# Linear attention and two feed-forward layers on one core: a new order of the second products, copies and accumulating transfers dealt out anew

## The chip, the core and the metric

The kernel runs on one core of a Trainium2 chip, in one launch. The metric is the time of an execution on the device in microseconds (us), lower is better. "Before" and "after" are the same program but for the change below. Engines are named as the profile names them: PE is the matrix engine (PEld its weight loads), DVE the vector engine, ACT the scalar engine, POOL and SP the other two; PSUM is the memory that PE writes its products to, SBUF the on-chip working memory.

## The reference

```
kv  = einsum('bhsd,bhse->bhde', k, v)          # B=8, H=8, S=576, D=64
att = einsum('bhsd,bhde->bhse', q, kv)
x   = att / sqrt(mean(att^2) + 1e-6) * g_norm  # -> x: 4608 tokens x 512
h   = x @ w_in ; x = (relu(h)^2) @ w_out       # layer 1: 512 -> 2048 -> 512
h   = x @ w_in2; out = (h * cos(h)) @ w_out2   # layer 2: 512 -> 2048 -> 512
```

All inputs and the output are float32; the four weight matrices come as 64-bit floats, read as pairs of 32-bit words and rebuilt as float32 on the chip.

## The kernel before

**Numbers in two parts.** A float32 operand of a large product is split into a rounded high part h (an ACT cast) and a low part l (a DVE subtraction). A product is then three matmuls: h·h, h·l and l·h.

**Two phases.** In the first phase (`run_chunks`, 72 chunks) attention is computed and half of layer 1's hidden width goes through plain products (L379, L416); the partial results go to memory as `p_d` through `evict` (L402, L404). All this time the weights of the rest are rebuilt (`load_w`, `conv_steps`), combined and written back to memory as `wi_d` and `ws_d`. The rest, half of layer 1 (m=0) and all of layer 2 (m=1), runs in the second phase (`run_slots`) as 30 **slots** (m, t, q): t is one of five token tiles (twice 512, 512, 512, 384, 384 tokens), q a group of hidden columns (2 groups in layer 1, 4 in layer 2). Slots 0 to 9 are layer 1, 10 to 29 layer 2; slots 6 to 9 and 22 to 29 have the narrow tiles of 384.

**Seven products instead of eight.** Each slot does a 2x2 block product with seven multiplications twice: seven **first products** (`first_product`, L508, input times w_in, banks FA and FB) and, after the activation (`relu_*` or `cos_*`), seven **second products** (`second_product`, L631, activation times w_out, banks SA and SB). Sums that several result blocks share are built in PSUM by leaving a bank standing: with the products called 0 to 6, block (0,0) is 0+1, (1,1) is 0+3+2+5, (0,1) is 0+3+2+4, (1,0) is 0+3+5+6. Products 0, 3, 5, 6 use one bank pair, 1, 2, 4 the other; which is SA and which SB alternates from slot to slot (`s_bank`).

**Second products before.** The order is `S_ORDER` = 0, 1, 3, 2, 5, 4, 6. In a "seeded" slot (26 of 30, `seeded_s`) product 0 isn't added to its result block; ACT copies its bank into the other bank (L650) and product 1 accumulates on top of that. `drain_product` takes the sums out of PSUM into the block's running sum in SBUF: by an ACT copy where the sum starts (L654), by a DVE addition (L662), or, in layer 2 but for the last slot, for the products in `BY_DMA` = 4, 5, 1, 6 by an ACT copy into a tile `part` (L659, pool `t`, two buffers) and an **accumulating transfer** issued from POOL's queue (L660).

**What sets the order.** Everything is emitted by one planner: `at(position, function, ...)` puts a step at a position counted in slots, `PH` = 1/7 slot being one product's place. First products of slot k run at k to k+1, second products at k+1.25 to k+2.25, one matmul of each in turn. `s_block` prepares the operand of second product i 1.6 places ahead (differences on DVE at L591, cast L607 on ACT, low part L608 on DVE); `x_block` does the same for the first products (L463, L481, L482), once per tile, around the start of slots with q=0; `late_stream` places seven conversions of layer 2's weights ("pairs": L111 to L125, L175, L192, L194). Each engine does its instructions in the order in which they were emitted. A tile waits until the earlier tile in the same place has been used; the pools of the second phase (`c`, `t`, `late`) lie where buffers of the first phase were.

Of the kernel before, what the change touches and what calls it, by code (L numbers as in the profile page):

```python
# [8 lines left out]
F32 = mybir.dt.float32  # L9
# [13 lines left out]
def kernel(  # L23
# [105 lines left out]
    def load_w(kind, m, f, i):  # L129
        if kind == "seven":  # L130
            raw = pools["raw"].tile([P, 4, P, 2], U32, tag="raw", name="raw")
            for df, places in ((0, (1, 0)), (1, (2, 3))):
                src = (wA, wB)[m][2 * f + df, :, 1, :].rearrange("p (c n) -> p c n", n=2 * P)
                for d, place in enumerate(places):
                    nc.sync.dma_start(out=raw[:, place].rearrange("p n two -> p (n two)"), in_=src[:, 2 * d + i, :])
        elif kind == "pair":
            raw = pools["raw"].tile([P, 4, P, 2], U32, tag="raw", name="raw")
            for df, dst in ((0, raw[:, 1:3]), (1, raw[:, 0::3])):
                src = (wA, wB)[m][2 * f + df, :, 0, :].rearrange("p (c n) -> p c n", n=2 * P)
                nc.sync.dma_start(out=dst.rearrange("p k n two -> p k (n two)"), in_=src[:, i::2, :])  # L140
        elif kind == "pairs":
            raw = pools["raw"].tile([P, 4, 2 * P, 2], U32, tag="raw", name="raw")
            for df, dst in ((0, raw[:, 1:3]), (1, raw[:, 0::3])):
                src = (wA, wB)[m][2 * f + df, :, 0, :].rearrange("p (k n) -> p k n", n=4 * P)
                nc.sync.dma_start(out=dst.rearrange("p k n two -> p k (n two)"), in_=src)
        else:
            if i:
                raw = x_p.tile([P, DM, 2], U32, tag="xr", name="raw", bufs=2)
            else:
                raw = pools["raw"].tile([P, DM, 2], U32, tag="raw", name="raw")  # L150
            nc.sync.dma_start(out=raw.rearrange("p n two -> p (n two)"), in_=(wA, wB)[m][f, :, i, :])
        raws[kind, m, f, i] = raw
# [271 lines left out]
    ORDER = (0, 1, 3, 2, 5, 4, 6)  # L424
    W_OF = (0, 1, 3, 4, 6, 5, 2)
    BLOCKS = {(0, 0): 2, (1, 1): 5, (0, 1): 6, (1, 0): 7}
    S_ORDER = (0, 1, 3, 2, 5, 4, 6)
    BY_DMA = (4, 5, 1, 6)
    SEEDED = 2

    def seeded(k):
        return k >= SEEDED and TILES[slots[k][1]][1] <= TILES[slots[k - 1][1]][1]

    def seeded_s(k):
        return seeded(k) and k < len(slots) - 1

    HOLD = 9
    xb, wi, ws, kept, hs, ys, sums, quads = {}, {}, {}, {}, {}, {}, {}, {}
# [83 lines left out]
    def t_tile(k, dtype, name):  # L522
        return big("c", dtype, name, TILES[slots[k][1]][1])
# [62 lines left out]
    def s_block(k, i):  # L586
        m, t, q = slots[k]
        b11, b12, b21, b22 = (ys.get((k, b)) for b in ((0, 0), (0, 1), (1, 0), (1, 1)))

        def minus(out, x, y):  # L590
            nc.vector.tensor_tensor(out=out, in0=x, in1=y, op=ALU.subtract)  # L591
            return out

        if i == 3:
            ys[k, "t1"] = minus(t_tile(k, F32, "t"), b12, b11)
            ys[k, "t2"] = minus(t_tile(k, F32, "t"), b22, ys[k, "t1"])
        src = {
            0: lambda: b11,
            1: lambda: b21,
            2: lambda: ys[k, "t1"],  # L600
            3: lambda: ys[k, "t2"],
            4: lambda: b22,
            5: lambda: minus(b12, b22, b12),
            6: lambda: minus(b21, b21, ys[k, "t2"]),
        }[i]()
        gs[k, i] = h, l = [t_tile(k, F32R, f"g{n}") for n in "hl"]
        nc.scalar.copy(out=h, in_=src)  # L607
        nc.vector.tensor_tensor(out=l, in0=src, in1=as32(h), op=ALU.subtract)  # L608

    def blocks_of(t, x, m=1):  # L610
        if m == 0:
            return x[:, :, :TILES[t][1]]
        return x.rearrange("p c n -> p (c n)").rearrange("p (b n) -> p b n", n=2 * P)[:, :TILES[t][1] // P]

    def s_bank(k, i):
        return psum[("SA", "SB")[(k + (i in (1, 2, 4))) % 2]]

    def second_product(k, i):
        m, t, q = slots[k]
        ps = blocks_of(t, s_bank(k, i), m)  # L620
        w, g = ws.pop((k, i)), gs.pop((k, i))
        nb = TILES[t][1] // P if m else 2
        for b in range(nb):
            n = 0
            for pp in range(2):
                for x, y in ((0, 0), (0, 1), (1, 0)):
                    if m == 0:
                        lhs, rhs = w[:, x, pp, b, :], g[y][:, pp, :]
                    else:
                        lhs, rhs = g[y][:, pp, b * P:(b + 1) * P], w[:, x, pp, :, :].rearrange("p i n -> p (i n)")  # L630
                    nc.tensor.matmul(  # L631
                        ps[:, b, :],
                        lhs,
                        rhs,
                        start=(n == 0 and (m == 0 or b % 2 == 0) and (i in (0, 2) or i == 1 and not seeded_s(k))),
                        stop=(n == 5),
                        skip_group_check=True,
                    )
                    n += 1
                    if n == 6 and b == nb - 1:  # L640
                        drain_product(k, i)
                    yield
# [3 lines left out]
    def drain_product(k, i):  # L646
        m, t, q = slots[k]
        ps, (d, j) = blocks_of(t, s_bank(k, i), m), SUM_OF[i]
        if i == 0 and seeded_s(k):
            nc.scalar.copy(out=blocks_of(t, s_bank(k, 1), m), in_=ps)  # L650
            return
        if q == 0 and m and i in (1 if seeded_s(k) else 0, 2, 3, 6):
            sums[m, t, d, j] = e = w_p.tile([P, 2, 512], F32, tag="w", name="sum")
            nc.scalar.copy(out=blocks_of(t, e), in_=ps)  # L654
        else:
            e = blocks_of(t, sums[m, t, d, j], m)
            if m and i in BY_DMA and k < len(slots) - 1:
                part = blocks_of(t, temp([P, 2, 512], F32, "part"))
                nc.scalar.copy(out=part, in_=ps)  # L659
                nc.gpsimd.dma_start(out=e, in_=part, accum_op=ALU.add)  # L660
            else:
                nc.vector.tensor_tensor(out=e, in0=ps, in1=e, op=ALU.add)  # L662
        if q == groups_of[m][-1] and i in (4, 5, 1, 6):
            t0, ht = TILES[t]
            if m == 0:
                later(0.1, nc.sync.dma_start, out=y_d[t][:, j, 2 * d:2 * d + 2, :], in_=e)
                return
            dst = out[t0 + j * ht:t0 + (j + 1) * ht, 2 * P * d:2 * P * (d + 1)]
            delay = 0.25 if k < len(slots) - 1 else 0
            later(delay, nc.sync.dma_start, out=dst.rearrange("(b p) n -> p b n", p=P), in_=e)  # L670
# [58 lines left out]
    w_stream.place(w_at, 0.5, range(2 * NH - NRAW, 2 * NH - NRAW + 2))  # L729
    late_stream = Stream(load_w, conv_w, [("pairs", 1, p, 0) for p in range(1, 2 * NP)])  # L730
    at(pos(0.15), late_stream.advance)
    late_stream.place([pos(0.45 + 1.05 * k) for k in range(5)] + [pos(9.9), pos(10.85)], 0)

    kv_stream = Stream(load_kv, kv_mm, [(b, c) for b in range(B) for c in range(NSC)])
    starts = [(-13, 1), (-3, 0.8)] + [(-3 + 7 * (b - 1), 7 / (2 * NKC)) for b in range(2, B)]
# [24 lines left out]
    for k, (m, t, q) in enumerate(slots):  # L760
# [6 lines left out]
            at(pos(k + (f - 2.7) * PH) if k or f > 2 else nA0 - 5 + f / 2, load_wi, k, i)  # L767
        for f, i in enumerate(S_ORDER):
            at(pos(k + LAG2 + (f - 2.7) * PH), load_ws, k, i)
            at(pos(k + LAG2 + (f - (1.1 if f == 1 else 1.6)) * PH), s_block, k, i)  # L770
        if not seeded(k):
            at(pos(k + 1 * PH), keep, k, "m1", 0)
            at(pos(k + 2 * PH), add, k, (0, 0), 1, "m1")
# [8 lines left out]
        chain = (cos_1, cos_2, cos_3, cos_4, cos_5) if m else (relu_1, relu_2)  # L782
        for b, f in BLOCKS.items():
            for a, fn in enumerate(chain):
                at(pos(k + (f + 0.25 * (a + 1)) * PH), fn, k, b)
        if m == 0 and q == 0:
            for n, dj in enumerate(((0, 0), (1, 1), (0, 1), (1, 0))):
                at(pos(k + LAG2 + (n - 2) * PH), load_sum, k, *dj)
# [36 lines left out]
    def run_slots():  # L825
        nonlocal here
        size = [42 * (TILES[t][1] // P if m else 2) for m, t, q in slots]

        def held(x):
            return 2 * PH - (2 * PH - x) * (12 - HOLD) / 12 if PH <= x < 2 * PH else x  # L830

        seconds = [
            k + LAG2 + (held(n / size[k]) if seeded_s(k) else n / size[k])
            for k in range(len(slots))
            for n in range(size[k])
        ]
        firsts = [(k, i) for k in range(len(slots)) for i in ORDER]
        steps1 = (x for k, i in firsts for x in first_product(k, i))
        todo = [(k, i) for k in range(len(slots)) for i in S_ORDER]
# [35 lines left out]
    with ExitStack() as early:  # L875
# [2 lines left out]
            return early.enter_context(tc.tile_pool(name=name, bufs=bufs, side="right"))  # L878

        right("pad", 1).tile([P, 56], F32, name="pad")  # L880
        pools["raw"] = right("conv", 2)
        x_p, g_p, ev_p, pools["t"] = (right(n, b) for n, b in (("x", XB), ("g", 3), ("ev", 2), ("tmp", 8)))
        with tc.tile_pool(name="att", bufs=1, side="right") as att_p:
            kvx = [att_p.tile([P, NKC, P], F32, tag=f"kvx{b}", name=f"kvx{b}") for b in range(2)]
            for x in kvx:
# [14 lines left out]
    ps_p = ctx.enter_context(tc.tile_pool(name="ps", bufs=1, space=PSUM))  # L900
    psum.update({n: ps_p.tile([P, 2, 512], F32, name=n) for n in ("FA", "FB", "SA", "SB")})
    pools["c"] = ctx.enter_context(tc.tile_pool(name="c", bufs=18, side="left"))
    pools["t"] = ctx.enter_context(tc.tile_pool(name="t", bufs=2, side="left"))
    pools["raw"] = ctx.enter_context(tc.tile_pool(name="late", bufs=1, side="left"))
    run_slots()


# [40 lines left out]
```

## Time and profile before

| | |
|---|---|
| median of three executions | 1594.57 us (lowest 1592.75) |
| profiled execution, its own time | 1593.9 us |
| its span in the trace | 1592.1 us |
| PE busy | 1542.6 us, 97% |
| PEld busy | 1349.8 us, 85% |
| DVE busy | 1254.8 us, 79% |
| ACT busy | 1107.7 us, 70% |
| POOL busy | 105.5 us, 7% |
| moved by DMA | 433.13 MB, 272 GB/s |

The span is the time from the first to the last instruction of the profiled execution. An engine's busy time says how much work it had; whether a millisecond is lost is read from the waits of the engine that is nearly always busy, here PE.

### The profile page before, as it was taken

The page shows a single profiled execution, that of the slowest core. Times are in us where ns is not written, and L with a number is a line of the kernel's source. Part 1 is how long each engine was busy: PE and PEld are TensorE (multiplying, and loading weights), DVE is VectorE, ACT ScalarE, POOL GpSimd, SP SyncE. Part 2 cuts the span into 40 slices and gives each one's busy share as a digit, 9 for nine tenths or more (in the row PEclk, how much of TensorE's full clock was granted, in tenths as well). Part 3 has the DMA queues.
Part 4 walks back from the last instruction along what each step waited for, and adds up shares of the span by engine and source line. Part 5 has one row for each costly group of instructions (what it writes and reads, how often), then busy time and mean ns, then how long its engine had stood idle before and what let it go on. Part 6 is the DMA issues. An engine that isn't in the chain of part 4 may idle for free.

```text
span 1592.1 us, 24817 instructions
## 1 busy us (share of the span) xinstructions
PE 1542.6 (97%) x9104; PEld 1349.8 (85%) x9104; DVE 1254.8 (79%) x1676; ACT 1107.7 (70%) x1568; POOL 105.5 (7%) x117
## 2 busy tenths in 40 slices
PE   5999999999999999999999999999999999999997
PEld 4777777778887777888998899999998999999997
DVE  7988788788885898987879868766876687687576
ACT  6977677775444666665656778877887777778774
POOL 1100101111000000000000000000000001011010
PEclk9999999999999999999999999999999999999999
DMA  9758889866678989998999779987998799999994
GB/s 325 269 168 230 261 259 284 238 204 208 195 230 298 309 283 338 319 385 263 336 355 341 279 229 269 280 266 227 268 271 263 227 262 297 333 302 275 323 296 116
DMA packets 229160, 433.13 MB, mean 272 GB/s; under 512 B 18608, under 2 KB 144816, under 8 KB 229040
## 3 DMA queue, kind: packets, MB, share of 16 engines
q1 hardware_dynamic: 218624, 397.21, 74.2%
q0 software_dynamic: 10416, 34.35, 10.7%
q8 instruction: 72, 1.18, 0.3%
q14 instruction: 48, 0.39, 0.1%
HBM read 317.72 MB, written 81.79 MB: 251 GB/s over the span
## 4 chain that ended last, share of the span: by engine, by line
PE 77%; DMA 8%; DVE 6%; issue 4%; ACT 4%; SPq 0%; DVEq 0%; ACTq 0%; POOLq 0%
PE SB L631 14%; PE SA L631 14%; PE FB L508 13%; PE FA L508 13%; PE acc L416 10%; PE l L379 9%; DMA sum<-part 2%; PE o L379 1%; DMA ws_d<-raw 1%; PE ss L379 1%; DVE gl L608 1%; DMA xraw<-x_d 1%; DMA q<-in_qT 1%; DMA p_d<-ev 1%; DMA raw<-in_wA 1%
## 5 line engine op out<-in xcount | busy, mean ns | idle before, releaser
L508 PE MATMUL FA<-xh,wi 128*128 128x512 f32 (+1 forms) x840 | 300.0, 371 | 8.0 <-ACT h L545 3.3
L508 PE MATMUL FB<-xh,wi 128*128 128x512 f32 (+1 forms) x840 | 299.3, 370 | 0.0
L631 PE MATMUL SA<-ws,gh 128*128 128x256 f32 x1008 | 230.3, 282 | 5.5 <-ACT gh L607 5.5
L631 PE MATMUL SB<-ws,gh 128*128 128x256 f32 x1008 | 229.3, 282 | 2.0 <-ACT SB L650 1.9
L631 PEld LDWEIGHTS SA<-ws,gh 128*128 128x128 f32 x1008 | 181.9, 190 | 17.3 <-ACT gh L607 6.2
L631 PEld LDWEIGHTS SB<-ws,gh 128*128 128x128 f32 x1008 | 181.0, 189 | 14.0 <-ACT SB L650 3.3
L508 PEld LDWEIGHTS FA<-xh,wi 128*128 128x128 f32 x840 | 157.3, 188 | 20.5 <-ACT h L545 3.9
L575 DVE SCALAR_TENSOR_TENSOR y<-y,h 128x1024 f32<-128x1024 f32 (+1 forms) x80 | 89.3, 1116 | 108.4 <-ACT y L571 108.1
L508 PEld LDWEIGHTS FB<-xh,wi 128*128 128x128 f32 x840 | 157.3, 188 | 11.1
L631 PE MATMUL SB<-ws,gl 128*128 128x256 f32 x504 | 142.4, 282 | 1.5 <-DVE gl L608 1.5
L631 PE MATMUL SA<-ws,gl 128*128 128x256 f32 x504 | 142.4, 282 | 0.6 <-DVE gl L608 0.6
L608 DVE TENSOR_TENSOR gl<-y,gh 128x1024 fp32r<-128x1024 f32 (+1 forms) x100 | 111.2, 1113 | 34.7 <-ACT gh L607 33.5
L660 POOL DMA_DIRECT2D sum<-part x67 | 57.0, 851 | 1101.9 <-DMA wi<-wi_d 535.2
L557 ACT ACTIVATE y<-h,zerob 128x1024 int32<-128x1024 f32 (+1 forms) x80 | 85.3, 1066 | 40.7 <-DVE h L533 40.6
L416 PE MATMUL acc<-gh,wh 128*128 128x512 f32 x288 | 113.6, 395 | 0.0
L416 PE MATMUL acc<-gl,wh 128*128 128x512 f32 x288 | 112.8, 392 | 0.0
L416 PE MATMUL acc<-gh,wl 128*128 128x512 f32 x288 | 112.6, 391 | 0.0
L508 PE MATMUL FA<-xl,wi 128*128 128x512 f32 (+1 forms) x300 | 111.3, 371 | 0.0
L508 PE MATMUL FB<-xl,wi 128*128 128x512 f32 (+1 forms) x300 | 110.9, 370 | 0.0
L607 ACT CAST gh<-y 128x1024 fp32r<-128x1024 f32 (+1 forms) x100 | 95.0, 962 | 12.6 <-DVE y L575 7.4
L631 PE MATMUL SB<-gh,ws 128*128 128x512 f32 (+1 forms) x280 | 100.0, 370 | 2.9 <-ACT SB L650 1.1
L631 PEld LDWEIGHTS SB<-ws,gl 128*128 128x128 f32 x504 | 95.5, 190 | 7.8 <-DVE gl L608 2.4
(172 smaller groups left out, 3775.4 us busy)
## 6 DMA issues: line engine op xcount, KB each, us to landing
wi<-wi_d SPq DMA_DIRECT2D x210, 512.0 KB, 6.8
ws<-ws_d SPq DMA_DIRECT2D x210, 512.0 KB, 6.0
sum<-part POOLq DMA_DIRECT2D x43, 512.0 KB, 8.1
kvld<-in_kv SPq DMA_DIRECT2D x32, 512.0 KB, 6.7
ws_d<-raw SPq DMA_DIRECT2D x24, 448.0 KB, 4.1
q<-in_qT SPq DMA_DIRECT2D x32, 288.0 KB, 4.0
p_d<-ev SPq DMA_DIRECT2D x18, 512.0 KB, 3.8
sum<-part POOLq DMA_DIRECT2D x24, 384.0 KB, 7.9
```

What stands on the lines that cost most here:

```text
L379: nc.tensor.matmul(ps, a[:, 0, cs], m[:], start=(c == 0 and k == 0), stop=(c == NKC - 1 and k == 2))
L416: nc.tensor.matmul(o, a[:, cs], m[:], start=(f == 0 and n == 0), stop=(f == NH - 1 and n == 2), skip_group_check=True)
L508: nc.tensor.matmul(ps[:, pp, :], a, b, start=(n == 0 and (i in (0, 2) or i == 1 and not seeded(k))), stop=(n == 5), skip_group_check=True,)
L557: nc.scalar.activation(out=y.bitcast(I32), in_=hs[k, b], func=AF.Identity, bias=zerob)
L575: nc.vector.scalar_tensor_tensor(out=y, in0=y, scalar=-2.0 * math.pi, in1=hs.pop((k, b)), op0=ALU.add, op1=ALU.mult)
L607: nc.scalar.copy(out=h, in_=src)
L608: nc.vector.tensor_tensor(out=l, in0=src, in1=as32(h), op=ALU.subtract)
L631: nc.tensor.matmul(ps[:, b, :], lhs, rhs, start=(n == 0 and (m == 0 or b % 2 == 0) and (i in (0, 2) or i == 1 and not seeded_s(k))), stop= ...
L660: nc.gpsimd.dma_start(out=e, in_=part, accum_op=ALU.add)
```

## The change

The order of the second products becomes 0, 2, 3, 4, 5, 1, 6, with no copy from bank to bank: product 0 is drained into block (0,0) in every slot, and products 0, 1 and 2 each start their bank afresh. `seeded_s` and the delay of the second products that it brought (`held`) go. `BY_DMA` becomes 2, 4, 1. The difference t1 is built with product 2's operand instead of product 3's, all operands are prepared 1.6 places ahead, and for block (1,0) the last three steps of the cosine come 0.3 places later. Five conversions of `late_stream` get other positions. `load_w` of kind "seven" issues three transfers instead of four for the same bytes. In SBUF the pool `ev` is placed ahead of `conv` (so pool `c` no longer lies on `ev`), and `late` ahead of `t` (so `late` lies on `conv`, `t` on `ev`).

```diff
-            for df, places in ((0, (1, 0)), (1, (2, 3))):
+            for df, d, n, place in ((0, 0, 1, 1), (0, 1, 1, 0), (1, 0, 2, 2)):
                 src = (wA, wB)[m][2 * f + df, :, 1, :].rearrange("p (c n) -> p c n", n=2 * P)
-                for d, place in enumerate(places):
-                    nc.sync.dma_start(out=raw[:, place].rearrange("p n two -> p (n two)"), in_=src[:, 2 * d + i, :])
+                dst = raw[:, place:place + n].rearrange("p k n two -> p k (n two)")
+                nc.sync.dma_start(out=dst, in_=src[:, 2 * d + i::2, :][:, :n])
...
-    S_ORDER = (0, 1, 3, 2, 5, 4, 6)
-    BY_DMA = (4, 5, 1, 6)
+    S_ORDER = (0, 2, 3, 4, 5, 1, 6)
+    BY_DMA = (2, 4, 1)
...
-    def seeded_s(k):
-        return seeded(k) and k < len(slots) - 1
...
+        if i == 2:
+            ys[k, "t1"] = minus(t_tile(k, F32, "t"), b12, b11)
         if i == 3:
-            ys[k, "t1"] = minus(t_tile(k, F32, "t"), b12, b11)
             ys[k, "t2"] = minus(t_tile(k, F32, "t"), b22, ys[k, "t1"])
...
-                        start=(n == 0 and (m == 0 or b % 2 == 0) and (i in (0, 2) or i == 1 and not seeded_s(k))),
+                        start=(n == 0 and (m == 0 or b % 2 == 0) and i in (0, 1, 2)),
...
-        if i == 0 and seeded_s(k):
-            nc.scalar.copy(out=blocks_of(t, s_bank(k, 1), m), in_=ps)
-            return
-        if q == 0 and m and i in (1 if seeded_s(k) else 0, 2, 3, 6):
+        if q == 0 and m and i in (0, 2, 3, 6):
...
-    late_stream.place([pos(0.45 + 1.05 * k) for k in range(5)] + [pos(9.9), pos(10.85)], 0)
+    late_stream.place([pos(n) for n in (0.95, 2.5, 3.25, 4.5, 6.4, 9.95, 10.85)], 0)
...
-            at(pos(k + LAG2 + (f - (1.1 if f == 1 else 1.6)) * PH), s_block, k, i)
+            at(pos(k + LAG2 + (f - 1.6) * PH), s_block, k, i)
...
-                at(pos(k + (f + 0.25 * (a + 1)) * PH), fn, k, b)
+                late = 0.3 if f == 7 and a > 1 else 0
+                at(pos(k + (f + late + 0.25 * (a + 1)) * PH), fn, k, b)
...
-        seconds = [
-            k + LAG2 + (held(n / size[k]) if seeded_s(k) else n / size[k])
...
+        seconds = [k + LAG2 + n / size[k] for k in range(len(slots)) for n in range(size[k])]
...
-        pools["raw"] = right("conv", 2)
-        x_p, g_p, ev_p, pools["t"] = (right(n, b) for n, b in (("x", XB), ("g", 3), ("ev", 2), ("tmp", 8)))
+        ev_p, pools["raw"] = right("ev", 2), right("conv", 2)
+        x_p, g_p, pools["t"] = (right(n, b) for n, b in (("x", XB), ("g", 3), ("tmp", 8)))
...
+    pools["raw"] = ctx.enter_context(tc.tile_pool(name="late", bufs=1, side="left"))
     pools["t"] = ctx.enter_context(tc.tile_pool(name="t", bufs=2, side="left"))
-    pools["raw"] = ctx.enter_context(tc.tile_pool(name="late", bufs=1, side="left"))
```

## Rows read from the trace of the kernel before

**Rows 1.** The page: busy time of PE; PE's granted clock in 40 slices.

```profile
PE 1542.6 (97%) x9104; PEld 1349.8 (85%) x9104; DVE 1254.8 (79%) x1676; ACT 1107.7 (70%) x1568; POOL 105.5 (7%) x117
...
PEclk9999999999999999999999999999999999999999
```

**Rows 2.** PE's waits: line, releaser: us in total, times, longest us.

```profile
PE SA L631 <- ACT gh L607: 5.5, 3, 3.5
PE ss L316 <- DVE m L329: 4.4, 3, 1.5
PE FA L508 <- ACT h L545: 3.3, 1, 3.3
PE SB L631 <- ACT SB L650: 3.0, 3, 1.5
PE FA L508 <- ACT m L527: 2.8, 2, 1.4
```

**Rows 3.** ACT's timeline, slot 27: start, us, engine, line [idle before <-releaser].

```profile
1476.50 0.80 ACT L659 COPY part<-SB 128x768 f32<-128x768 f32 x1 [4.88 <-DMA sum<-part]
...
1480.68 0.80 ACT L545 ACTIVATE h<-FA 128x768 f32<-128x768 f32 x1
```

**Rows 4.** Stretches: length, busy PE, PEld, DVE, ACT, POOL, clock, DMA share, GB/s.

```profile
503.30:561.30 58.00, 54.09 (x235) 43.75 (x236) 45.38 (x47) 35.26 (x37) 0.00 (x0) 1.00 0.93 308
561.30:716.30 155.00, 152.80 (x672) 125.35 (x671) 144.62 (x142) 98.85 (x103) 0.00 (x0) 1.00 0.94 333
...
914.80:1309.20 394.40, 394.04 (x2522) 356.71 (x2521) 295.76 (x256) 305.24 (x312) 29.70 (x35) 1.00 0.87 256
1344.10:1530.40 186.30, 181.29 (x1273) 180.01 (x1272) 131.03 (x145) 142.45 (x186) 17.03 (x20) 0.99 0.97 307
...
1480.00:1500.00 20.00, 18.46 (x121) 18.46 (x122) 15.20 (x17) 15.53 (x21) 0.00 (x0) 0.91 0.97 350
...
1571.00:1575.00 4.00, 3.92 (x18) 3.71 (x18) 2.80 (x5) 2.09 (x3) 0.00 (x0) 0.57 0.00 0
```

**Rows 5.** Accumulating transfers (L660), issue to landing; the page's row of the narrow ones.

```profile
DMA to landing us min/median/max: 3.8/8.1/11.7
...
sum<-part POOLq DMA_DIRECT2D x24, 384.0 KB, 7.9
```

**Rows 6.** Groups of instructions by form: one drain of each kind, full width.

```profile
L662 DVE TENSOR_TENSOR sum<-SB,sum 128x1024 f32<-128x1024 f32 x28 | 34.1, 1220 | 11.3 <-PE SB L631 11.3
...
L659 ACT COPY part<-SB 128x1024 f32<-128x1024 f32 x22 | 22.3, 1012 | 14.6 <-PE SB L631 9.5 <-DMA sum<-part 5.1
...
L650 ACT COPY SA<-SB 128x1024 f32<-128x1024 f32 x8 | 8.0, 1001 | 5.8 <-PE SB L631 5.7
```

**Rows 7.** The last slots: ACT's and PE's timelines, the chain, DVE's timeline.

```profile
1562.96 0.81 ACT L659 COPY part<-SB 128x768 f32<-128x768 f32 x1
...
1570.08 0.38 PE L631 MATMUL SA<-ws,gh 128*128 128x256 f32 x1 [3.52 <-ACT gh L607]
1571.07 0.54 PE L631 MATMUL SA<-ws,gl 128*128 128x256 f32 x1 [0.61 <-DVE gl L608]
...
1575.97 0.35 PE L631 MATMUL SA<-ws,gh 128*128 128x256 f32 x1 [0.98 <-ACT gh L607]
...
1581.14 2.16 PE SB L631 x18
...
1587.65 0.96 DVE L662 TENSOR_TENSOR sum<-SB,sum 128x768 f32<-128x768 f32 x1 [1.20 <-PE SB L631]
```

**Rows 8.** The chain and ACT's timeline where the first phase ends.

```profile
503.30 4.93 DMA p_d<-ev
...
508.41 1.05 ACT xh L481
...
509.36 1.02 ACT L527 ACTIVATE m<-FA 128x1024 f32<-128x1024 f32 x1
```

**Rows 9.** Issues of the "seven" loads from layer 2's weights: ns min/median/max.

```profile
L135 SPq DMA_DIRECT2D raw<-in_wB x64: 328/423/1035, 194.0 to 365.8; - x64
```

More of the change, by code (lines that the diff above doesn't have):

```diff
@@ L827, in run_slots @@
         size = [42 * (TILES[t][1] // P if m else 2) for m, t, q in slots]
-        def held(x):
-            return 2 * PH - (2 * PH - x) * (12 - HOLD) / 12 if PH <= x < 2 * PH else x
-        seconds = [
-            k + LAG2 + (held(n / size[k]) if seeded_s(k) else n / size[k])
-            for k in range(len(slots))
-            for n in range(size[k])
-        ]
+        seconds = [k + LAG2 + n / size[k] for k in range(len(slots)) for n in range(size[k])]
         firsts = [(k, i) for k in range(len(slots)) for i in ORDER]
```

## The prediction

> **What bounds the kernel now.** I read the page's busy times first. PE is busy for 97% of the span and its granted clock is at the upper level, 2.4 GHz, nearly everywhere [rows 1]. No matmul is added or taken away, so what can be won is PE's idle time, 1592.1 - 1542.6 = 49.5 us in all, and the little that a lowered clock costs. Next come PE's waits, each with its releaser [rows 2]: they show that the second phase loses little in any one place. Then I read the stretches of the slots [rows 4]. In slots 12 to 21 (914.8 to 1309.2 us) PE is busy for 394.04 of 394.40 us: nothing is left there. The losses sit in four places: slots 0 and 1 (54.09 busy of 58.00), slots 2 to 5 (2.2 us), slots 23 to 28 (181.29 of 186.30) and the tail behind the last first product [rows 7]. So this is a PE-bound kernel, and the change can only take away or add single waits.
>
> **The change part by part.** The sum is made against the profiled execution, 1593.9 us, 0.7 us below the median of 1594.57.
>
> *Copies in PSUM.* 26 ACT copies L650 of 1.0 us go [rows 6]. They sat between product 0 and product 1 in consecutive places, and PE waited for them 3.0 us in three cases [rows 2]. In the new order each drain has a whole place of another product before its bank is wanted again, so **-3.0**. Bounds: -3.0, and 0 if the DVE drain that replaces the copy is just as late.
>
> *Accumulating transfers.* In layer 2's seeded slots with q from 1 on, ACT had five copies a slot and DVE two drains; now ACT has three and DVE four. ACT was busy for 305 and DVE for 296 of 394 us in slots 12 to 21 [rows 4]; two drains of 1.22 us [rows 6] in three of four slots of 39.4 us raise DVE from 75% to about 80%: hidden. The transfers stood in the places 1, 4, 5, 6 and now stand in 1, 3, 5. `part` has two buffers, and one transfer needs 7.9 us in the narrow slots [rows 5], where a place is about 4.3 us (186.3 us less 5.0 us of waits, over 42 places, rows 4). Three in a row must wait; every second place, 8.6 us, is just enough. That is the wait of 4.88 us of ACT ahead of a `part` copy at 1476.5 us, which held back the drain L545 and with it PE for 3.3 us [rows 2, 3]; the clock fell to a mean of 0.91 for the next 20 us, worth 20 x 0.09 = 1.8 us [rows 4]. Together **-5.1** (bounds -5.1 and 0).
>
> *What is late next.* Block (0,0) now gets product 1 by transfer in place 5, and product 0 of the next slot by DVE two places later. The addition reads what the transfer writes, so DVE waits for its landing. Narrow slots: 0.5 (the copy's turn on ACT, an estimate: it stands among steps of 0.8 us, so half of one is ahead of it [rows 3, 7]) + 0.8 + 7.9 = 9.2 us against 8.6: DVE stands for some 0.6 us in six slots, with everything queued behind it. PE needs the bank again for product 3 at 12.9 us, and the drain is done at 9.2 + 0.96 = 10.2 [rows 7]: covered. In the wide slots two places are 11.3 us against 0.5 + 1.0 + 8.1 = 9.6: no wait. I take **+1** for the splits behind it (bounds 0 and, at the longest landing of 11.7 us, 6 x 1.1 = 7). The Trainium skill (DMA: Bandwidth & Descriptors, Anatomy of one DMA) gives a transfer from POOL's queue as about 2.0 us plus its bytes over 436 GB/s, an estimate of 2.9 us for 384 KB; by that there would be no wait at all and this term were 0. No landing in this trace was under 3.8 us and the median is 2.7 times the figure [rows 5], so the trace decides.
>
> *The tail.* The last slot's product 1 came second and needed block (1,0), whose cosine chain ends last; PE stood 3.5 us for its cast, 0.6 for its low part and 1.0 for the next cast, and the clock fell to 0.57, so that 18 matmuls took 3.92 us where the same number takes 2.16 at full clock [rows 4, 7]. That is 5.1 + 1.8 = 6.9 us. Now product 1 is sixth. Late next is product 0's drain, which waits for the transfer of slot 28's product 1. This product stands where product 4 stood, whose copy ended at 1563.8 us [rows 7]; with 3.8 to 7.9 us to landing [rows 5] and 0.96 us the drain is done between 1568.5 and 1572.6. Product 0 ended at 1566.6, product 2 lasts until 1568.7, then product 3 wants the bank: a wait of 0 to 3.9 us. I take 3.0 with a dip of the clock: **-3.9** (bounds 0 and -6.9).
>
> *Buffers.* At the end of the first phase ACT's cast into a tile of `c` waits for the last `p_d` transfer, which lands at 508.2 us because that tile lies on `ev`; the drain of FA queued behind it holds PE 1.4 us [rows 2, 8]. Now `c` lies on buffers whose last readers are matmuls that end at about 501 us: **-1.4**. `t` takes over `ev`, but its first use is half a slot later. Bounds -1.4 and +1.
>
> *Conversions.* The one at 1.5 slots moves out of the x blocks of slot 2, where its steps on DVE and ACT stood between theirs. FA's other wait for L527, 1.4 us [rows 2], was in that place. I take **-1.0** (bounds -1.4 and +3, the conversion at 0.95 pushing other steps). In slots 2 to 5 three conversions remain, and each slot gets one more DVE drain: 144.6 + 4 x 1.22 = 149.5 of 152.8 us of PE time [rows 4]. That is the thinnest cover of the whole change; if it is gone, the price is these 4.9 us.
>
> *Loads.* 24 items with one issue less, 0.42 us each on SP's queue [rows 9], 10 us of SP in the first phase, with the same bytes. PE's largest waits there are for DVE's step L329, 4.4 us [rows 2]; SP's issue is off that chain most of the time. I take 0 (bounds -2 and +2).
>
> *New small waits.* PE's order changes in all 30 slots, and the trace shows waits of 0.4 to 1.5 us at single products; I add **+1.5**.
>
> Sum: -3.0 - 5.1 + 1 - 3.9 - 1.4 - 1.0 + 0 + 1.5 = -11.9, so 1593.9 - 11.9 = **1582.0 us**, 0.7% faster.
>
> **Rivals.**
> - *The waits only move.* Each of them has a neighbour almost as late: DVE is at 93% in slots 2 to 5, DMA at 0.97 in slots 23 to 28 [rows 4], and half of the gains hang on one wait each. For it: the tail, where I could name the successor. Against: the copies and the three transfers in a row really go. Time: 1590 to 1596, between 4 us of the 11.9 that remain and 2 us that are added.
> - *The transfer of product 1 becomes the bound (slower).* The place is product 0's drain in the 15 slots with q from 1 on. PE stands as soon as a landing takes over 12.9 - 0.5 - 0.8 - 0.96 = 10.6 us in the narrow slots (six) or 16.9 - 0.5 - 1.0 - 1.2 = 14.2 us in the wide ones (nine). At 15 us it costs 6 x 4.4 + 9 x 0.8 = 34 us, against gains of about 15: 1613 us; at 12.5 us, 6 x 1.9 = 11, about 1590. For it: the longest landing is 11.7 us already and DVE would block all its other work. Against: transfers fall from four to three a slot, evenly spaced, and the median is 8.
> - *DVE becomes the bound in layer 1's wide slots.* One drain more in each; 5 to 10 us of PE waits there eat most of the gain: 1587 to 1592. For it: 93%. Against: the conversions leave the fullest stretch.
> - *All waits of the slots go.* Tail 6.9, slot 27 5.1, copies 3.0, slots 0 and 1 3.9, single waits about 4 (the rest of 49.5 us lies in the start and in attention): 23 us, 1571. The Trainium skill (Perfetto Trace Analysis, Identifying the Most-Contended Engine) holds that matmul busy time says little of the distance to the roof and that the weight loads' share does; at 85% [rows 1] more than 3% would be open. The stretch of slots 12 to 21 shows PE without a gap at a fixed matmul count, and nothing here changes the matmuls, so I give this way no more than that.
>
> **How the numbers follow.** Forecast (1575 to 1588) 0.52; waits only move 0.22; DVE in layer 1 0.09; transfer of product 1 0.09, half of it above 1600; all waits go 0.08. The time is that of the likeliest case, 1582. The range leaves out the upper half of the slow case and a part of the fastest: **1572 to 1598**. A measurement can tell about 2% from no change, here 32 us. Faster by that would be under 1562.7, more than all the waits of the slots together: 0.03. Slower by it is over 1626, which takes landings of over 15 us in all slots: 0.04. Within: 0.93.
>
> **What would show it.** Right: no wait of PE for a copy from bank to bank; no wait of ACT ahead of `part` of over 1 us; FA's first drain at about 503 instead of 509 us; in the tail one wait at product 3 of the last slot, for DVE's drain L662, of under 4 us; DVE's waits for `sum<-part` about 1 us each in narrow slots; a span of about 1580. Wrong: PE waiting for L662 in many slots with a transfer behind it, DVE without a gap through slots 2 to 5 with PE waiting for L608 or L537, or the first phase (to 503 us) shifted by more than 2 us.

## The result, and the profile after

The changed kernel takes 1577.04 us (median of four, 1574.25 to 1579.28) against 1593.87 for the kernel before (median of four, one of them a slow execution of 6261.2 us, which the ratio leaves out); the ratio is 0.9896, with a 95% interval of 0.9872 to 0.9920. Timed again later it was 0.9872 (0.9854 to 0.9891). So the change gains about 1.1%; 1582 was forecast. The profiled execution took 1579.28 us, the longest of the four, with a span of 1577.5; the steps below are told against it.

Page of the kernel after, busy times [rows 1 before]:

```profile
PE 1538.8 (98%) x9104; PEld 1348.9 (86%) x9104; DVE 1293.7 (82%) x1717; ACT 1074.1 (68%) x1527; POOL 93.6 (6%) x102
```

PE has the same matmuls; DVE has 39 us more and ACT 34 less. PE's idle time went from 49.5 to 38.7 us. PE's waits after (line, releaser: us in total, times, longest), where L505 is the old L508, L629 the old L631, L605 the old L607, L606 the old L608, L524 the old L527, L654 and L657 the old L659 and L662 [rows 2 before]:

```profile
PE ss L316 <- DVE m L329: 7.6, 4, 3.7
PE l L379 <- ACT r L388: 3.2, 3, 2.1
...
PE SA L629 <- ACT gh L605: 1.0, 1, 1.0
...
PE SB L629 <- issue: 0.9, 1, 0.9
PE FA L505 <- ACT ev L402: 0.8, 1, 0.8
PE SB L629 <- ACT part L654: 0.6, 1, 0.6
PE SA L629 <- DVE sum L657: 0.5, 1, 0.5
```

The waits for a copy from bank to bank, for L542 (the old L545) and for L524 are gone. What remains in the slots is under 1.1 us each; the 1.0 and 0.9 us at L629 stand where layer 2 begins, a stretch in which the kernel before had 1.0 and 0.8 us. But the first phase got worse: the wait for L329 rose from 4.4 to 7.6 us. The same stretches of slots as in [rows 4]: length, busy PE, PEld, DVE, ACT, POOL, clock, DMA share, GB/s; each begins with the first matmul of slot 0, 2, 12 and 23.

```profile
509.90:562.60 52.70, 52.70 (x233) 43.65 (x234) 44.40 (x43) 35.92 (x38) 0.00 (x0) 1.00 0.91 317
562.60:715.00 152.40, 152.40 (x673) 126.06 (x672) 145.16 (x143) 94.44 (x96) 0.00 (x0) 1.00 0.92 329
...
913.40:1306.10 392.70, 392.70 (x2522) 356.28 (x2521) 313.87 (x273) 289.12 (x296) 23.79 (x28) 1.00 0.83 249
1340.90:1520.40 179.50, 178.95 (x1273) 178.66 (x1273) 139.25 (x156) 135.05 (x176) 13.60 (x16) 1.00 0.94 307
```

PE is without a gap in three of the four. The second phase begins at 509.9 us instead of 503.3 (+6.6) and lasts 1067.6 us instead of 1088.8 (-21.2); together -14.6, which is 1593.9 - 1579.3. By slots, from the first matmul of one to that of another: slots 0 to 9 take 328.3 us instead of 336.0 (-7.7), slots 10 and 11 the same (-0.2), slots 12 to 29 636.2 instead of 645.2 (-9.0, of which slot 27 is -5.1 and slot 23 -1.8), the tail, from the start of the last first product's last matmul, 27.9 instead of 32.1 (-4.3).

### The profile page after: what moved, and what is told of

The parts are those of the page before. It is cut to its first block, busy times and chain, and to the rows that moved or that the text cites. A ratio compares the mean times of both kernels' runs of the same rounds, so it can differ in the third digit from the quotient of the medians.

```text
span 1577.5 us, 24643 instructions
## 1 busy us (share of the span) xinstructions
PE 1538.8 (98%) x9104; PEld 1348.9 (86%) x9104; DVE 1293.7 (82%) x1717; ACT 1074.1 (68%) x1527; POOL 93.6 (6%) x102
## 4 chain that ended last, share of the span: by engine, by line
PE 84%; DMA 5%; DVE 5%; ACT 3%; issue 2%; SPq 0%; POOL 0%; DVEq 0%; ACTq 0%; POOLq 0%
PE FA L505 16%; PE SB L629 16%; PE FB L505 15%; PE SA L629 15%; PE acc L416 10%; PE l L379 8%; DMA ws_d<-raw 1%; PE o L379 1%; PE ss L379 1%; DMA q<-in_qT 1%; DMA sum<-part 1%; DMA raw<-in_wB 1%; DMA xraw<-x_d 1%; DVE gl L606 1%; DMA kvld<-in_kv 1%
## 5 line engine op out<-in xcount | busy, mean ns | idle before, releaser
L505 PE MATMUL FA<-xh,wi 128*128 128x512 f32 (+1 forms) x840 | 302.0, 370 | 0.8 <-ACT ev L402 0.8
L505 PE MATMUL FB<-xh,wi 128*128 128x512 f32 (+1 forms) x840 | 301.8, 370 | 0.0
L629 PE MATMUL SA<-ws,gh 128*128 128x256 f32 x1008 | 233.3, 280 | 1.9 <-ACT gh L605 1.0
L629 PE MATMUL SB<-ws,gh 128*128 128x256 f32 x1008 | 233.2, 280 | 1.1 <-ACT part L654 0.6
L629 PEld LDWEIGHTS SA<-ws,gh 128*128 128x128 f32 x1008 | 183.6, 188 | 14.8 <-ACT gh L605 2.0
L629 PEld LDWEIGHTS SB<-ws,gh 128*128 128x128 f32 x1008 | 183.3, 188 | 13.2 <-ACT part L654 0.8
L505 PEld LDWEIGHTS FA<-xh,wi 128*128 128x128 f32 x840 | 157.1, 188 | 10.7 <-ACT ev L402 1.2
L505 PEld LDWEIGHTS FB<-xh,wi 128*128 128x128 f32 x840 | 157.2, 188 | 9.6
L629 PE MATMUL SB<-ws,gl 128*128 128x256 f32 x504 | 141.4, 281 | 0.5 <-DVE gl L606 0.5
L606 DVE TENSOR_TENSOR gl<-y,gh 128x1024 fp32r<-128x1024 f32 (+1 forms) x100 | 111.2, 1113 | 37.2 <-ACT gh L605 37.1
L629 PE MATMUL SA<-ws,gl 128*128 128x256 f32 x504 | 141.2, 280 | 0.5 <-DVE gl L606 0.5
L505 PE MATMUL FA<-xl,wi 128*128 128x512 f32 (+1 forms) x300 | 111.0, 370 | 0.0
L505 PE MATMUL FB<-xl,wi 128*128 128x512 f32 (+1 forms) x300 | 110.9, 370 | 0.0
L655 POOL DMA_DIRECT2D sum<-part x52 | 44.3, 851 | 1094.8 <-ACT part L654 992.8
L564 ACT ACTIVATE y<-y 128x1024 f32<-128x1024 f32 (+1 forms) x80 | 78.1, 976 | 37.4 <-DVE y L558 37.2
L629 PE MATMUL SB<-gh,ws 128*128 128x512 f32 (+1 forms) x280 | 101.0, 369 | 0.9 <-issue 0.9
L379 PE MATMUL l<-xh,wh 128*128 128x512 f32 x240 | 97.3, 406 | 4.4 <-ACT r L388 3.2
```

Of the source, the lines that this page charges most:

```text
L379: nc.tensor.matmul(ps, a[:, 0, cs], m[:], start=(c == 0 and k == 0), stop=(c == NKC - 1 and k == 2))
L505: nc.tensor.matmul(ps[:, pp, :], a, b, start=(n == 0 and (i in (0, 2) or i == 1 and not seeded(k))), stop=(n == 5), skip_group_check=True,)
L564: nc.scalar.activation(out=y, in_=y, func=AF.Sin, scale=math.pi)
L629: nc.tensor.matmul(ps[:, b, :], lhs, rhs, start=(n == 0 and (m == 0 or b % 2 == 0) and i in (0, 1, 2)), stop=(n == 5), skip_group_check=True,)
```

## The experiments

The second phase repeats itself closely: from its first matmul it took 1067.6 us in the profile of the changed kernel and 1068.7 in a second one, so edits there can be read to about 1 us from stretches. The kernel before is less steady: its slots 0 to 9 took 336.0 us in its own profile, but 336.5 and 338.4 us in two of the edited ones below (three loads; `BY_DMA` without 4), whose instructions in these slots come in the same order; nearly all of the difference is in slot 0 (20.9 to 23.4 us). The moment at which the second phase starts isn't steady either; it has a pair of experiments of its own.

**1. The loads of kind "seven", undone in the changed kernel, and done alone in the kernel before.** The edit is the first hunk of the change, backward and forward.

```diff
-            for df, d, n, place in ((0, 0, 1, 1), (0, 1, 1, 0), (1, 0, 2, 2)):
+            for df, places in ((0, (1, 0)), (1, (2, 3))):
```

> The changed kernel with the old four transfers per item of the kind 'seven' (one edit undone). The changed kernel's profile reached its first product 6.6 us later than before (509.9 against 503.3 us), with one new wait of 3.5 us at 297.8 us. Theory A (the loads are worth nothing, the shift is a matter of when transfers happen to land): the first product again anywhere between 502 and 511 us, the time within 3 us of the changed kernel's 1577. Rival B (three transfers of which one is twice as long delay the conversions): first product at about 503 us, time about 1570.5.

> The kernel before with only the new three transfers per item of the kind 'seven'. Theory A: 1594 within 3 us. Rival B: first product at about 510 us and 1600 us.

With four transfers the changed kernel took 1573.60 us (1573.28 to 1574.22; ratio to before 0.9858, 0.9843 to 0.9873). Three transfers in the kernel before gave a ratio of 1.0014 (1.0002 to 1.0026), 1598.71 against 1596.59 us. First product of the second phase in the profiles (the row's first start), changed kernel with four, then kernel before with three:

```profile
L505 PE MATMUL FA<-xh,wi x840: 333/389/499, 503.0 to 1538.4; 128*128 128x512 f32 x102, 128*128 128x384 f32 x66
```

```profile
L508 PE MATMUL FA<-xh,wi x840: 333/389/522, 506.3 to 1561.7; 128*128 128x512 f32 x102, 128*128 128x384 f32 x66
```

In the profiles of the other kernels here it came at 501.1 to 503.4 us with four (four profiles) and at 503.8 to 509.9 with three (seven profiles). So rival B is right in direction, and the loads cost some 2 us (0.3 to 4.2 by the interval of the second test), more in single executions. My term of 0 was wrong. Rival B's own numbers, 510 us and 1600 us, weren't reached by the kernel before: 506.3 and 1598.7.

**2. Why three transfers are slower.** PE's new wait at 298 us, then the chain of waits of the changed kernel around it (start, length, what):

```profile
PE ss L316 <- DVE m L329: 3.7, 1, 3.7
```

```profile
285.66 3.16 DMA raw<-in_wB
289.67 2.59 DMA ws_d<-wh
292.27 0.51 ACT wh L192
...
296.34 3.95 DMA xraw<-x_d
301.36 0.47 DVE m L329
```

A load of x (L227) is issued at 296.3, behind the "seven" loads; ACT's cast L232 waits for it with L321 queued behind, DVE's L329 waits for that, and PE for DVE. With four transfers the same load is issued at 286.9, ahead of the "seven" loads. The edit of one transfer had changed the order of a few instructions on SP, ACT and DVE at four places of the first phase, near 190, 210, 250 and 290 us. The positions given to `at` are the same in both kernels, so they alone don't fix the order on the queues. Behind the wait the clock fell:

```profile
301.30:304.70 3.40, 2.83 (x8) 2.35 (x9) 3.27 (x5) 2.27 (x6) 2.49 (x2) 0.50 0.17 52
```

That is worth about 1.4 us more (half of PE's 2.83 busy us, an estimate). All eight profiles with three transfers and this order have the wait, of 0.6 to 3.7 us; none of the five with four transfers has it. In the six where the clock fell behind it the second phase began at 506.3 to 509.9 us, in the two where it didn't at 503.8 us. So I kept three transfers and moved only the x load of that tile.

```diff
-            at(n0 - (4 if t == NDIRECT else 5.2) + q, load_x, t, q)
+            at(n0 - (4 if t == NDIRECT else 5.8 if t == 5 else 5.2) + q, load_x, t, q)
```

> The changed kernel (three transfers per 'seven' item) with the load of x for token tile 5 placed 0.6 chunks earlier, which puts it ahead of the 'seven' loads on SP's queue near 290 us. Theory O (the three transfers cost time in the first phase because the planner's order on SP changes, and the x load of tile 5, late behind them, blocks ACT's cast L232 and with it PE for 3.5 us): that wait of PE near 298 us is under 1 us, the first product at 503 to 506 us, the time about 1573 to 1575. Rival P (the transfers themselves are slower, whatever their order): first product scattered from 504 to 510 us as before, 1577.

```profile
L505 PE MATMUL FA<-xh,wi x840: 333/389/498, 503.0 to 1538.5; 128*128 128x512 f32 x102, 128*128 128x384 f32 x66
```

In its profile PE has no wait between 280 and 310 us and the second phase begins at 503.0, where the unedited kernel beside it had a wait of 3.1 us and began at 509.6. That is theory O for this wait. But the time it forecast, 1573 to 1575 us, was not reached: the four timed runs scatter from 1572.2 to 1577.1 us with a median of 1575.71, the same as the unedited kernel's 1575.68: other waits of the first phase stay. That the order is all of the loads' price is not shown.

> The changed kernel once more, without an edit, beside the two that follow. All theories: 1574 to 1580 us; the first product of the second phase between 503 and 510 us, the second phase from there 1067 to 1069 us.

It took 1575.68 us; its profile began the second phase at 509.6 us and needed 1068.7 us from there, all as expected.

**3. The pools, undone** (`t` is opened ahead of `late` again, too).

```diff
-        ev_p, pools["raw"] = right("ev", 2), right("conv", 2)
-        x_p, g_p, pools["t"] = (right(n, b) for n, b in (("x", XB), ("g", 3), ("tmp", 8)))
+        pools["raw"] = right("conv", 2)
+        x_p, g_p, ev_p, pools["t"] = (right(n, b) for n, b in (("x", XB), ("g", 3), ("ev", 2), ("tmp", 8)))
...
```

> The changed kernel with both pool placements of before (c on ev again, late on x). Theory A (each edit pays its own wait): slot 0 waits again for the last transfer of partial sums, the first drain of FA moves about 4 to 5 us behind the first product's start, slots 0 and 1 get 1.5 to 2 us longer, nothing else changes: about 1579. Rival C (the buffers don't matter because ACT or DVE is late there anyway): 1577 with slots 0 and 1 as in the changed kernel.

The chain of waits at the start of the second phase:

```profile
508.44 4.93 DMA p_d<-ev
...
514.50 1.03 ACT m L524
```

PE's waits there:

```profile
PE FA L505 <- issue: 2.3, 1, 2.3
PE FA L505 <- ACT m L524: 1.4, 1, 1.4
```

The wait for the last `p_d` transfer is back, as in [rows 8]: slots 0 to 9 take 330.0 us, +1.7. Theory A, by the stretch; in time, 1580.46 us and a ratio of 0.9896, it is lost in the scatter of the first phase.

**4. The positions of the conversions, undone.**

```diff
-    late_stream.place([pos(n) for n in (0.95, 2.5, 3.25, 4.5, 6.4, 9.95, 10.85)], 0)
+    late_stream.place([pos(0.45 + 1.05 * k) for k in range(5)] + [pos(9.9), pos(10.85)], 0)
```

> The changed kernel with the old positions of the seven weight conversions. The two profiles differ by 3.6 us in the stretch of slot 1 and 0.9 us in slot 2. Theory A (the conversion at 1.5 slots stood among the x blocks and made PE wait for ACT's drains L524 and L537 there): waits of 2.5 to 4.5 us in slots 1 to 3 come back, about 1581. Rival D (these waits came with the old order of the second products and its copies): 1577, slots 1 and 2 without a wait.

PE's waits from 500 to 650 us:

```profile
PE FA L505 <- ACT ev L402: 0.8, 1, 0.8
PE FA L505 <- ACT m L524: 0.7, 1, 0.7
PE SB L629 <- ACT FB L537: 0.7, 1, 0.7
```

The first stands in the changed kernel too; the other two are new. Slots 0 to 9 take 330.4 us, +2.1: the two waits of 0.7 us and 0.7 us that no wait shows. Theory A in kind, but under the 2.5 to 4.5 us that it asked for; 1578.15 us.

**5. The copies in PSUM, taken out of the kernel before.**

```diff
     def seeded_s(k):
-        return seeded(k) and k < len(slots) - 1
+        return False
```

> The kernel before with the old order of the second products, but no copy from bank to bank: product 0 is drained into block (0,0) in every slot, product 1 starts its bank afresh, nothing is held back; transfers, pools, loads and positions as before. Theory A (the copies cost only what PE waited for them, 3.0 us in the profile before): about 1593 on a chip where before takes 1596, no wait for a copy. Rival E (the copies were the main cost, through ACT, whose queue they lengthened): 1585 or less, and the 3.3 us wait of PE for ACT's L545 near 1478 us gone as well. Rival F (product 1 in the second place needs block (1,0), which ends last; without the held places PE waits for its cast in many slots): 1600 or more.

1593.94 us against 1596.34, ratio 0.9980 (0.9967 to 0.9992): -2.4 us. PE's largest waits in its slots:

```profile
PE SA L631 <- ACT gh L607: 4.5, 3, 2.8
PE FA L508 <- ACT m L527: 3.5, 2, 2.1
PE SB L631 <- ACT gh L607: 2.3, 1, 2.3
```

The waits for the copies are gone and little else: slot 27 still takes 34.4 us, where ACT's wait for a transfer now reaches PE as the wait of 2.3 us for a cast, and the tail 32.0. Theory A, by the timed runs alone: in the profile the second phase is no shorter (1089.5 us against 1088.8), because slot 0 took 23.1 us instead of 20.9. Product 1 in the second place did not become a wait of every slot (rival F).

**6. Accumulating transfers: spaced in the old order, in a row in the new one.** In the kernel before, `BY_DMA` = (5, 1, 6); in the changed one, `BY_DMA` = (4, 5, 1, 6).

```diff
-    BY_DMA = (4, 5, 1, 6)
+    BY_DMA = (5, 1, 6)
```

> The kernel before, order and copies as they were, but product 4 of layer 2 drained by DVE, so that the accumulating transfers stand in the places 1, 4 and 6 instead of 1, 4, 5, 6: three a slot, no two in a row. Theory A (the 5.1 us near 1478 us come from transfers in a row that wait for one of two buffers): ACT's waits ahead of its part copies fall from 13.0 us to under 3, PE's wait of 3.3 us for L545 and the fall of the clock behind it go, the time is 4 to 6 us under before's. Rival R (the stall came with the old order and its copies; four transfers in a row in the new order did little harm): the stall stays, the time is within 2 us of before's.

> The changed kernel with the old set of products that go by accumulating transfer, 4, 5, 1, 6. In the new order these are four places in a row. Theory A (with two buffers, every transfer after the second in a row makes ACT wait until an earlier one has landed, and what stands behind it on ACT makes PE wait): ACT waits ahead of its part copies in most narrow slots, 2 to 6 us each, PE waits 3 us or more in several, time 1590 to 1615. Rival G (the wait near 1478 us was a chance meeting): 1577 within 3 us.

Old order with spaced transfers: 1591.24 against 1597.03 us, ratio 0.9965 (0.9951 to 0.9978). ACT's wait for a transfer ahead of `part` in the kernel before, its waits ahead of `part` with the edit, and slots 23 to 28 with a little beside them:

```profile
ACT part L659 <- DMA sum<-part: 13.0, 8, 4.9
```

```profile
ACT part L659 <- PE SB L631: 11.5, 9, 1.9
ACT part L659 <- PE SA L631: 8.6, 11, 1.3
```

```profile
1340.00:1526.00 186.00, 185.41 (x1315) 184.37 (x1315) 141.86 (x158) 142.31 (x184) 11.88 (x14) 1.00 0.93 302
```

No wait for a transfer is left (13.0 us in eight cases before), slot 27 takes 29.6 us instead of 34.7. That is the whole 5.1 us, with order and copies as they were: theory A. (The edit also takes 19 copies off ACT, so it isn't spacing alone.) The opposite test went the other way. Four in a row in the new order:

```profile
ACT part L654 <- DMA sum<-part: 6.3, 7, 2.6
```

```profile
1341.50:1523.50 182.00, 179.70 (x1273) 178.89 (x1272) 134.23 (x149) 139.66 (x182) 18.75 (x22) 1.00 0.99 316
```

ACT waits again, but 2.6 us at the longest, and PE loses 2.3 us in these slots (0.6 in the changed kernel); slot 27 takes 29.6 us, as in the changed kernel. The time is 1578.68 us, within rival G's 3 us of 1577 and far from the 1590 that theory A asked for. So in the new order spaced transfers aren't what keeps the stall away. A row of transfers makes ACT wait in both orders; the one that reached PE with 3.3 us in the kernel before followed a transfer of 10.2 us (the chain of waits there), and why the rows of four did so little harm is open.

**7. Product 1 drained by DVE.**

```diff
-    BY_DMA = (2, 4, 1)
+    BY_DMA = (2, 4)
```

> The changed kernel with product 1 of layer 2 drained by DVE instead of ACT and a transfer, so that product 0 of the next slot waits for no transfer. In the changed kernel's profile DVE stood 6.4 us in five cases for such a transfer. Theory A (these waits are covered and cost PE nothing): 1577 within 2 us, DVE's waits for part gone, DVE 15 drains of about 1 us busier. Rival H (the transfer of product 1 is what holds the tail and the narrow slots): faster by 2 to 4 us.

In the changed kernel DVE stood for transfers as feared; what ended the idle time before L657 (us, times), then the landings of the transfers L655:

```profile
  DMA sum<-part: 6.4, 5
```

```profile
DMA to landing us min/median/max: 3.8/7.2/10.9
```

Without them slots 23 to 28 look like this:

```profile
1335.00:1513.60 178.60, 178.60 (x1273) 178.60 (x1273) 144.46 (x162) 131.59 (x170) 8.51 (x10) 1.00 0.89 295
```

The second phase takes 1067.2 us against 1067.6, slots 23 to 28 0.9 us less, and the time is 1577.49 us: theory A, these waits cost PE under 1 us.

**8. The old order in the last slot alone** (its second operand is prepared 1.1 places ahead, as before the change).

```diff
+    def s_order(k):
+        return S_ORDER if k < len(slots) - 1 else (0, 1, 3, 2, 5, 4, 6)
```

> The changed kernel, but the last slot alone does its second products in the old order 0, 1, 3, 2, 5, 4, 6. Theory A (the tail's gain comes from product 1 standing sixth, because block (1,0) ends last): PE waits 3 us or more for the cast of product 1 behind the last first product, the clock falls, the tail grows from 28 to 31 or 33 us and the time by 3 to 5 us. Rival I (the tail got shorter because ACT no longer waits there for a buffer of part): tail as in the changed kernel, 28 to 29 us.

PE in the tail (start, length, instruction [idle before <-releaser]), and a stretch of it:

```profile
1561.34 0.58 PE L632 MATMUL SA<-ws,gh 128*128 128x256 f32 x1 [4.94 <-ACT gh L608]
1562.33 0.58 PE L632 MATMUL SA<-ws,gl 128*128 128x256 f32 x1 [0.41 <-DVE gl L609]
1567.42 0.55 PE L632 MATMUL SA<-ws,gh 128*128 128x256 f32 x1 [0.88 <-ACT gh L608]
```

```profile
1561.00:1566.00 5.00, 4.25 (x18) 3.96 (x19) 3.66 (x4) 2.11 (x4) 0.00 (x0) 0.50 0.00 0
```

Up to the last first product this profile is the changed kernel's to 0.1 us; then the tail takes 35.1 us instead of 27.9. The picture of [rows 7] is back, the fall of the clock with it: 1582.83 us, ratio 0.9905. Theory A, and more than it asked for. In the changed kernel the same stretch has five short waits, and in this profile the clock stays at 1.00:

```profile
1556.68 0.35 PE L629 MATMUL SA<-ws,gh 128*128 128x256 f32 x1 [0.35 <-ACT y L564]
1557.50 0.39 PE L629 MATMUL SA<-ws,gl 128*128 128x256 f32 x1 [0.46 <-DVE gl L606]
1560.29 0.35 PE L629 MATMUL SB<-ws,gh 128*128 128x256 f32 x1 [0.50 <-ACT gh L605]
1561.16 0.35 PE L629 MATMUL SA<-ws,gh 128*128 128x256 f32 x1 [0.51 <-DVE sum L657]
1561.97 0.38 PE L629 MATMUL SB<-ws,gl 128*128 128x256 f32 x1 [0.47 <-DVE gl L606]
```

In the second profile of the same kernel (2) the same five waits, of 0.35 to 0.51 us, were followed by the lower clock, and the tail took 29.1 us. The stretch behind them, here and then there:

```profile
1562.50:1565.90 3.40, 3.40 (x30) 3.40 (x30) 2.75 (x4) 1.57 (x2) 0.00 (x0) 1.00 0.00 0
1562.10:1565.50 3.40, 3.40 (x19) 3.40 (x18) 1.53 (x3) 1.56 (x2) 0.00 (x0) 0.50 0.00 0
```

Of the seven profiles with this tail (the two here and those of (3), (4), (9), of four transfers in (1) and of the early x load in (2)) four show that fall and take 29.0 to 29.1 us; three don't and take 27.7 to 27.9.

**9. A version that beats both.** Four transfers, and the last two conversions away from the place where layer 2 begins.

```diff
-    late_stream.place([pos(n) for n in (0.95, 2.5, 3.25, 4.5, 6.4, 9.95, 10.85)], 0)
+    late_stream.place([pos(n) for n in (0.95, 2.5, 3.25, 4.5, 6.4, 10.5, 11.6)], 0)
```

> The changed kernel with the old four transfers per 'seven' item, and the last two weight conversions moved from 9.95 and 10.85 to 10.5 and 11.6 slots, away from the place where layer 2 begins and PE waits 0.9 + 1.0 us. Theory A: these two waits go, 1571 to 1573 us where the changed kernel takes 1577. Rival Q (the waits are the cosine chain's own and stay): 1573.6 as with the four transfers alone.

1570.49 us (1567.62 to 1572.31), ratio 0.9837 (0.9818 to 0.9856), beside 1575.68 for the changed kernel; some 2 us of that belong to the four transfers (1). Slots 10 and 11:

```profile
831.40:904.00 72.60, 72.60 (x403) 64.81 (x402) 66.80 (x67) 53.64 (x57) 0.91 (x1) 1.00 0.84 299
```

PE has no gap there; these two slots take 72.7 us instead of 75.2. Theory A: the waits were the conversions', not the cosine chain's.

## Why the prediction was right

The forecast of 1582 us and its range held, by its own mechanism: a PE-bound kernel from which single waits go. Its sum of -11.9 us stands against -14.6 in the profiled execution, and that is made of larger gains in the second phase (-21.2) and a loss in the first (+6.6) that I did not forecast. So it was in part luck that the total came so near: two misses of opposite sign. One of my own signs of being wrong, a first phase shifted by more than 2 us, came true in this execution.

- *Copies in PSUM, -3.0.* Right within the noise: -2.4 us alone in the kernel before (5; 1.3 to 5.3 by the interval).
- *Accumulating transfers, -5.1.* Right in size: slot 27 is 5.1 us shorter. The cause is settled by half: in the old order it is enough to take product 4 off the transfers (6), but the new order gets rid of the stall even with four in a row, which cost it only 2.3 us in the narrow slots. "Three in a row must wait" was too strong, and what in the new order does it is not shown.
- *What is late next, +1.* DVE did stand for product 1's transfer, 6.4 us in five cases, and it was covered but for under 1 us (7). The landings' median even fell from 8.1 to 7.2 us. The estimate of 2.9 us for 384 KB from the Trainium skill (DMA: Bandwidth & Descriptors, Anatomy of one DMA) stays far off.
- *The tail, -3.9.* -4.3 here and -3.0 in the second profile. The cause is shown (8); what took its place isn't one wait of up to 3.9 us for the drain of product 0 but five of up to 0.5 us, one of them for a drain. The dip of the clock that I counted in came in some executions and not in others.
- *Buffers, -1.4.* -1.7 (3). FA's first drain starts 3.1 us after the first product instead of 6.0. (My sign, a drain at about 503 us, could not come: that is where the first product itself began before.)
- *Conversions, -1.0.* Half of what it was: +2.1 when undone (4).
- *Loads, 0.* Wrong: the bound of +2 was reached on the median and passed in single executions. I looked at SP's time per issue; what mattered in the one wait that (2) removed was the place of another load on SP's queue, which the edit had shifted, and the fall of the clock behind that wait.
- *DVE in slots 2 to 5.* The thinnest cover held: DVE is busy for 145.2 us of 152.4 and PE has no gap. 149.5 was forecast.
- *New small waits, +1.5.* Too much: beside the tail the slots have one, of 0.6 us (for a `part` copy).

Slots 0 to 9 gained 7.7 us against the shortest of the old order's three profiles, more against the others. Undoing pools and conversions accounts for 3.8; the other 3.9 or more I put down to the new order of the second products (the copies alone gave nothing there in (5)), but no run isolates it.

Of the rivals, "the waits only move" fell with the list of PE's waits, in which no neighbour took over, "DVE becomes the bound" with the stretch of slots 2 to 5, and "the transfer of product 1 becomes the bound" with (7). "All waits of the slots go" came nearest: its price of 23 us for the second phase against 21.2 measured. I gave it 0.08, since I looked for a successor at every wait that went; in a stretch where each product has a whole place of lead there mostly was none.

## What to carry to other kernels

Where one engine is busy for 97% of the span, the ceiling of an edit is the list of that engine's waits: price each one, and then name the next-latest event; if the new order gives that event a whole product's time of lead, count the gain in full. Put what is ready last (here block (1,0)) to use last, above all in the tail, where nothing else fills the gap. And where the program's order is worked out by machine, an edit of one transfer can also move instructions around it: compare the order on each queue before pricing it as issues saved.

## What the runs showed of the hardware

A stop of 4.9 us of PE in (8) was followed by the lower clock level, 1.2 GHz, for some ten microseconds (0.50 granted from 1561 to 1570 us, and a mean of 0.94 over the next ten). Five stops of 0.35 to 0.51 us within six microseconds were followed by 3.4 us at that level in one profile of the changed kernel and by none in another, so one profile can't say what such stops cost: 19 matmuls went through in the 3.4 us at 0.50, 30 in as long at 1.00 (8). With fifteen accumulating transfers fewer, and none in consecutive places, the median landing was 7.2 us instead of 8.1; the longest, 10.9 us instead of 11.7, is no gain that lasts, since (3) had one of 12.0 us.
